# Convolution with generated weights, then a tanh-shrink MLP: a check of the softmax sums on chip, and a general version behind a branch

## The chip, the cores and the metric

The kernel runs on one core of a Trainium2 chip. A core has five engines with a queue of instructions each: PE (matrix multiply), DVE (vector), ACT (scalar and activation functions), POOL (general purpose) and SP (which here issues transfers). They run side by side and wait for each other through semaphores. The metric is the device time of one execution in microseconds; the profile is of one execution of its own.

## The reference

Per token and head, seven raw weights are turned into a softmax, which weighs the seven latest tokens of that head's channel group. The result goes through a two-layer MLP whose activation is h - tanh(h).

```python
batch, seq, d_model = (8, 4096, 192); kernel_size = 7; n_heads = 8; d_ff = 2048
x = randn(batch, seq, d_model) * 0.1
weight_gen = randn(batch, seq, n_heads, kernel_size) * 0.3

w = weight_gen - np.max(weight_gen, axis=-1, keepdims=True)
w = np.exp(w)
w = w / (np.sum(w, axis=-1, keepdims=True) + 1e-09)
x_pad = np.concatenate([np.zeros((B, pad, D)), x], axis=1)
x_unf = x_pad[:, idx, :].reshape(B, S, K, H, group)      # idx: the 7 latest tokens
out = np.einsum('bshk,bskhg->bshg', w, x_unf).reshape(B * S, D)
h = out @ w_in
g = h - np.tanh(h)
return g @ w_out                                          # (32768, 192) float32
```

## The kernel before

The 32768 tokens are cut into 32 superblocks of 1024 tokens (`TOK`), numbered n = 0 to 31. In a superblock each of the 128 partitions holds eight tokens in a row (`J = 8`). For each superblock:

1. `weight_gen` and `x` are loaded (`load_wg`, `load_x`, on SP's queue). `softmax_exp` takes the exponential in place on ACT. The row maximum of the reference is not subtracted.
2. `softmax_sum` (lines 179 to 187) adds the seven exponentials of each token and head on DVE into a tile `zsum`: 64 sums per partition and superblock, from 448 numbers; in the steady part it is done in two halves of 32 sums from 224 numbers. `softmax_recip`, `softmax_norm` and `softmax_norm_ramp` take reciprocals of them, also on DVE, and scale the exponentials.
3. `products` multiplies `x` with the weights, mostly on POOL, with DVE's help (`help`, lines 250 and 251). The seven products of a token are added partly by transfers with addition, partly by PE.
4. PE transposes and adds the products (`conv_sums`, line 384), and ACT copies the result to `convT` (line 410).
5. The first matrix multiply (`gemm1`, lines 422 to 445) runs over 16 f tiles of 128 of the 2048 hidden channels. For each f tile PE makes `ph` (line 427, six matmuls: three chunks of channels, two row halves of 64), ACT takes the tanh into `th` (line 440), and DVE subtracts into `gt`, in bfloat16 (line 441). `ph` lives in a PSUM pool of three buffers, `psum_h`; the transposes' `pc` and the last superblock's `po2` take slots of the same ring. `th` has three buffers too.
6. The second matrix multiply (`out_stream`, line 495) runs one superblock behind: its matmuls, in pairs of two row halves, are interleaved with the first's of the next superblock. How many pairs follow each f tile is written out in `plan["pairs"]` (`STEADY`, line 682). ACT copies the sums to `out_sb` (line 514) and SP stores a whole superblock at once (line 518).

After the last superblock's f tiles nothing is left to interleave with. `gemm2_last` (lines 529 to 559) then runs the second multiply of superblock 31 by itself, token block by token block (j = 0 to 7): 32 matmuls into a slot of `psum_h` (line 538), a copy of one half by ACT (line 551), an addition by DVE (line 552), and after every second block a store by SP (line 554).

All of this stands under `tc.manual_schedule()` (line 564): on each engine the instructions run in the order in which the program writes them. So the place of a call in the loop of lines 707 to 768 is its place in the engine's queue. In that loop f tile k of superblock n issues first `gemm1(n, k)`, with its subtraction on DVE; what a later line of the same pass puts on DVE runs after the subtraction of f tile k and before that of f tile k + 1. Sums, halves of sums and normalizations of a coming superblock are put into the passes n = 1 to 27; from n = 28 on there is no coming superblock left for which they would be done (`soft`, line 712, is empty).

`psum_h` and all other pools are entered on `ctx` and live until the kernel ends. The program has no branch.

Of the kernel before, what the change touches and what calls it, by code (L numbers as in the profile page):

```python
# [8 lines left out]
FP32 = mybir.dt.float32  # L9
BF16 = mybir.dt.bfloat16  # L10

ACT = mybir.ActivationFunctionType
AX = mybir.AxisListType


@with_exitstack
def kernel(
# [20 lines left out]
    JH = J // 2  # L38
    HT = TOK // 2
    NSB = S // TOK  # L40
    NTOT = B * NSB
    NFT = F // P
    NC = D // R
    KA, KH = 4, 2
    PART = (2, 3)
    TWO_SUMS = (13, 14, 15, 16, 17, 18, 19, 20, 21, 22, 23, 24, 25, 26, 27, 28, 29, 30, 31)
    AHEAD = 4
# [11 lines left out]
    assert NFT == 2 * J, "one token block of the second matmul per pair of f tiles"  # L59

    const = ctx.enter_context(tc.tile_pool(name="const", bufs=1))
    xpool = ctx.enter_context(tc.tile_pool(name="xpool", bufs=2))
    wgpool = ctx.enter_context(tc.tile_pool(name="wgpool", bufs=3))
    papool = ctx.enter_context(tc.tile_pool(name="papool", bufs=3))
# [113 lines left out]

    def softmax_sum(n, j0=0, j1=J):

        if j0 == 0:
            zsum_of[n] = wgpool.tile([P, J * H], FP32, name="zsum")
        nc.vector.reduce_sum(  # L183
            out=zsum_of[n][:, j0 * H : j1 * H],
            in_=e_of[n][:, j0:j1].rearrange("p j h k -> p (j h) k"),
            axis=AX.X,
        )

    def softmax_recip(n, j0=0, j1=J):
        if j0 == 0:  # L190
            zr_of[n] = wgpool.tile([P, J * H], FP32, name="zr")
        nc.vector.reciprocal(zr_of[n][:, j0 * H : j1 * H], zsum_of[n][:, j0 * H : j1 * H])

    def softmax_norm(n, bank):

        wsm = softmax_tile()
        zr_v = bank[:, 512 - J * H : 512]
        nc.vector.reciprocal(zr_v, zsum_of[n][:])  # L198

        def finish():  # L200
            scale(nc.vector, wsm[:], e_of[n], zr_v)

        wsm_of[n] = (wsm, None, None, None)
        return finish

    def softmax_norm_ramp(n, bank):

        softmax_sum(n)
        wsm = softmax_tile()
        zr_v = bank[:, 512 - J * H : 512]  # L210
        nc.vector.reciprocal(zr_v, zsum_of[n][:])  # L211
# [14 lines left out]
        wsm_of[n] = (wsm, wsm_v, None, None)  # L226

    def scale(eng, wsm, e_t, zr):
        return eng.tensor_mul(  # L229
# [248 lines left out]
    half = {}  # L478
# [50 lines left out]
    def gemm2_last(j, f0=0, f1=NFT):  # L529

        n = NTOT - 1
        if f0 == 0:
            half[j] = psum_h.tile([P, 2, HT], FP32, name="po2", tag="ph")
        po = half[j]
        col = (j % 2) * HT + (j // 2) * P
        for f in range(f0, f1):
            for r in range(2):
                nc.tensor.matmul(  # L538
                    po[:, r, 0:D],
                    lhsT=g_of[n][f][r * R : (r + 1) * R, col : col + P],  # L540
                    rhs=w_out[r * R : (r + 1) * R, f, :],
                    start=(f == 0),
                    stop=(f == NFT - 1),
                )
        if f1 < NFT:
            return
        if j == 0:
            out_of[n] = opool.tile([P, J, D], FP32, name="out_sb")
        out_sb = out_of[n]
        ot = tpool.tile([P, D], FP32, name="ot", tag="th")  # L550
        nc.scalar.activation(out=ot[:], in_=po[:, 0, 0:D], func=ACT.Copy)
        nc.vector.tensor_add(out_sb[:, j, :], po[:, 1, 0:D], ot[:])
        if j % 2 == 1:
            nc.sync.dma_start(
                out=out[n * TOK : (n + 1) * TOK, :].rearrange("(p j) e -> p j e", p=P)[
                    :, j - 1 : j + 1, :
                ],
                in_=out_sb[:, j - 1 : j + 1, :],
            )
# [147 lines left out]
    for n in range(1, NTOT):  # L707
        more = n < NTOT - 1
        finish = []
        plan = FIRST if n == 1 else DOUBLE if n in DOUBLE_IN else APART if n in APART_IN else STEADY  # L710

        soft = [m for m in (n + 3 if n <= AHEAD else n + 4,) if m < NTOT]
        for f in range(NFT):
            ph = gemm1(n, f)
            if n == 1:
                if f == 1:
                    load_wg(5)
                if f == 5:
                    softmax_exp(4)
                steps = ((softmax_sum, 3), (softmax_recip, 3), (softmax_sum, 4))  # L720
                for at, (step, m, h) in zip(plan["sums"], [s + (h,) for s in steps for h in (0, 1)]):
                    if f == at:
                        step(m, h * JH, (h + 1) * JH)
                if f == 5:
                    wsm_of[3] = (softmax_tile(), None, e_of[3], zr_of[3])
                    rest = products(3)
            elif f == 1:
                if soft:
                    softmax_exp(soft[0])
                if n + 2 < NTOT:  # L730
                    rest = products(n + 2)
            if n == AHEAD and f == 4:
                softmax_exp(n + 4)
            if n > 1:
                for h, at in enumerate(plan["sums"]):
                    if soft and f == at:
                        softmax_sum(soft[0], h * JH, (h + 1) * JH)
            if n == AHEAD:
                for at, (step, h) in zip(EXTRA, [(s, h) for s in (softmax_sum, softmax_recip) for h in (0, 1)]):
                    if f == at:  # L740
                        step(n + 4, h * JH, (h + 1) * JH)
                if f == EXTRA[-1]:
# [24 lines left out]
            if f == (9 if n == 1 else 1) and n <= STORE_FIRST:  # L767
                loads(n)
# [3 lines left out]
    gemm2_last(0, J, NFT)  # L772
    for j in range(1, J):
        gemm2_last(j)


# [28 lines left out]
```

## Time and profile before

| | us |
|---|---|
| median of 3 runs | 746.48 (745.1 to 747.17) |
| span of the profiled execution | 743.4 |
| PE busy in it | 722.3 (97%) |
| DVE busy | 687.4 (92%) |
| ACT busy | 638.8 (86%) |
| POOL busy | 654.5 (88%) |
| `gemm1`'s subtractions on DVE (line 441), 512 of 1.217 us | 601.6 |
| sums on DVE (line 183), 61 of 0.387 us in the mean | 23.6 |
| matmuls of the last superblock's second multiply (line 538), 256 | 11.2 |

The span runs from the first to the last instruction that the profile shows; the runs' device time also holds what lies around it. A line of the profile's list of groups names line, engine, operation, output<-inputs, shapes and count; then the busy time and the mean in ns of one; then the idle time of the engine just before these instructions and who ended most of it. "PEld" is the loading of weights into PE, which overlaps its matmuls. A name with a q, as SPq, is an engine's sequencer: it waits and issues, and the engine itself is not busy. The chain that ended last is followed backwards from the last instruction, at each step to what released it.

### The profile page before, as it was taken

The page shows a single profiled execution, that of the slowest core. Times are in us where ns is not written, and L with a number is a line of the kernel's source. Part 1 is how long each engine was busy: PE and PEld are TensorE (multiplying, and loading weights), DVE is VectorE, ACT ScalarE, POOL GpSimd, SP SyncE. Part 2 cuts the span into 40 slices and gives each one's busy share as a digit, 9 for nine tenths or more (in the row PEclk, how much of TensorE's full clock was granted, in tenths as well). Part 3 has the DMA queues.
Part 4 walks back from the last instruction along what each step waited for, and adds up shares of the span by engine and source line. Part 5 has one row for each costly group of instructions (what it writes and reads, how often), then busy time and mean ns, then how long its engine had stood idle before and what let it go on. Part 6 is the DMA issues. An engine that isn't in the chain of part 4 may idle for free.

```text
span 743.4 us, 30037 instructions
## 1 busy us (share of the span) xinstructions
PE 722.3 (97%) x13616; PEld 556.5 (75%) x13616; DVE 687.4 (92%) x723; ACT 638.8 (86%) x872; POOL 654.5 (88%) x163
## 2 busy tenths in 40 slices
PE   3899999999999999999999999999999999999997
PEld 2477777778777777777777777777777777877777
DVE  7999899999999999999999999999999999988893
ACT  4888888888888888989889999898998989888882
POOL 7999999999999999999999999999999999991000
PEclk9899999999999999999999999999999999999999
DMA  8925367766567668878777977877887877776112
GB/s 236 245 46 161 135 172 185 195 179 149 124 183 184 183 185 224 210 199 203 166 202 209 236 186 204 178 195 205 221 209 195 192 181 194 193 149 110 45 45 86
DMA packets 34269, 130.06 MB, mean 175 GB/s; under 512 B 4591, under 2 KB 9439, under 8 KB 30174
## 3 DMA queue, kind: packets, MB, share of 16 engines
q0 software_dynamic: 19424, 51.12, 40.4%
q1 hardware_dynamic: 14718, 77.03, 27.6%
q8 instruction: 106, 1.74, 0.9%
q14 instruction: 21, 0.17, 0.1%
HBM read 54.52 MB, written 25.17 MB: 107 GB/s over the span
## 4 chain that ended last, share of the span: by engine, by line
PE 92%; DVE 5%; ACT 1%; issue 1%; DMA 1%; SPq 0%; DVEq 0%
PE ph L427 43%; PE obank L495 43%; PE pc L384 4%; DVE gt L441 3%; PE po L538 1%; ACT th L440 1%; DVE pa L299 1%; DMA wg_t<-in_weight_gen_dram 1%; DVE zsum L183 0%; SPq L134 0%; ACT convT L402 0%; DVE obank L211 0%; DVE pa L251 0%; DVE pb L299 0%; SPq L144 0%
## 5 line engine op out<-in xcount | busy, mean ns | idle before, releaser
L441 DVE TENSOR_TENSOR gt<-ph,th 128x1024 bf16<-128x1024 f32 x512 | 601.6, 1217 | 33.4 <-ACT th L440 23.2
L440 ACT ACTIVATE th<-ph 128x1024 f32<-128x1024 f32 x512 | 512.1, 1025 | 69.2 <-PE ph L427 60.3
L427 PE MATMUL ph<-convT,w_in 64*128 64x512 bf16 x3072 | 415.1, 379 | 5.3 <-DVE gt L441 3.3
L495 PEld LDWEIGHTS <-gt 64*128 64x128 bf16 x7936 | 355.6, 94 | 80.6 <-issue 6.3
L495 PE MATMUL obank<-w_out,gt 64*128 64x192 bf16 x7936 | 408.0, 243 | 0.9 <-issue 0.8
L299 POOL TENSOR_TENSOR pa<-x_t,wsm 128x2688 bf16<-128x2688 f32 (+3 forms) x68 | 338.9, 5232 | 0.2
L299 POOL TENSOR_TENSOR pb<-x_t,wsm 128x4608 bf16<-128x4608 f32 (+2 forms) x33 | 283.8, 8601 | 0.7 <-ACT wsm L221 0.5
L427 PEld LDWEIGHTS <-w_in 64*128 64x128 bf16 x3072 | 163.0, 94 | 86.0 <-issue 18.3
L514 ACT ACTIVATE out_sb<-obank 128x192 f32<-128x192 f32 x248 | 81.3, 328 | 11.2 <-PE obank L495 10.3
L410 ACT ACTIVATE convT<-pc 128x1024 bf16<-128x1024 f32 (+1 forms) x62 | 50.1, 810 | 2.9 <-PE pc L384 2.7
L236 POOL DMA_DIRECT2D pa<-pb x28 | 36.0, 1284 | 13.7 <-POOL pb L299 9.1
L384 PEld LDWEIGHTS <-pa 64*128 64x128 bf16 x2064 | 41.5, 100 | 6.8 <-DVE pa L299 1.1
L236 POOL DMA_DIRECT2D pa<-pa x21 | 34.7, 1651 | 9.6 <-DMA pa<-pb 8.9
L384 PE MATMUL pc<-ident,pa 64*128 64x64 bf16 x1968 | 41.2, 191 | 1.8 <-POOL pa L299 0.9
L183 DVE TENSOR_REDUCE zsum<-wg_t 128x32 f32<-128x224 f32 (+1 forms) x61 | 23.6, 387 | 2.9 <-ACT wg_t L169 2.9
L169 ACT ACTIVATE wg_t<-wg_t 128x448 f32<-128x448 f32 x32 | 18.2, 570 | 6.3 <-DMA wg_t<-in_weight_gen_dram 6.2
L251 DVE TENSOR_TENSOR pa<-x_t,ph 128x384 bf16<-128x384 f32 x34 | 18.8, 554 | 2.0 <-DVE ph L250 0.3
L229 DVE TENSOR_TENSOR wsm<-wg_t,pc 128x448 f32<-128x448 f32 x27 | 16.8, 621 | 2.5
L198 DVE RECIPROCAL pc<-zsum 128x64 f32<-128x64 f32 x27 | 14.9, 550 | 0.0
L384 PE MATMUL pc<-ident,pb 64*128 64x64 bf16 x216 | 4.9, 206 | 9.0 <-POOL pb L299 9.0
L384 PEld LDWEIGHTS <-pb 64*128 64x128 bf16 x288 | 6.3, 106 | 9.5 <-POOL pb L299 9.0
L538 PE MATMUL po<-w_out,gt 64*128 64x192 bf16 x256 | 11.2, 243 | 0.0
(27 smaller groups left out, 56.8 us busy)
## 6 DMA issues: line engine op xcount, KB each, us to landing
x_t<-in_x_dram SPq DMA_DIRECT2D x31, 1344.0 KB, 7.9
pa<-pb POOLq DMA_DIRECT2D x28, 1152.0 KB, 9.5
out_dram<-out_sb SPq DMA_DIRECT2D x31, 768.0 KB, 3.9
pa<-pa POOLq DMA_DIRECT2D x21, 768.0 KB, 7.2
wg_t<-in_weight_gen_dram SPq DMA_DIRECT2D x32, 224.0 KB, 7.1
x_t<-in_x_dram SPq DMA_DIRECT2D x1, 768.0 KB
w_out<-in_moe_w_out_dram POOLq DMA_DIRECT2D x1, 768.0 KB, 9.5
out_dram<-out_sb SPq DMA_DIRECT2D x4, 192.0 KB, 3.0
```

Of the source, the lines that this page charges most:

```text
L183: nc.vector.reduce_sum(out=zsum_of[n][:, j0 * H : j1 * H], in_=e_of[n][:, j0:j1].rearrange("p j h k -> p (j h) k"), axis=AX.X,)
L236: return nc.gpsimd.dma_start(out=out.rearrange("p k j d -> p k (j d)"), in_=in_.rearrange("p k j d -> p k (j d)"), accum_op=mybir.AluOpTyp ...
L251: nc.vector.tensor_mul(pa[:, 0:KH, j, :].rearrange("p k (h g) -> p k h g", h=H), bass.AP(tensor=x_v.tensor, offset=x_v.offset + j * D, ap= ...
L299: return eng.tensor_mul(prod(k0, k1)[:, :, j0:j1].rearrange("p k j (h g) -> p k (j h) g", h=H), bass.AP(tensor=x_v.tensor, offset=x_v.offs ...
L384: nc.tensor.matmul(pc[r][:, col : col + R] if home else pc[:, r, col : col + R], lhsT=prods[c][gi][r * R : (r + 1) * R, 2 * j : 2 * j + 2] ...
L410: last_conv[0] = nc.scalar.activation(out=out, in_=pc[:, :, 0:cols].rearrange("p r (cj t) -> p r cj t", t=R), func=ACT.Copy,)
L427: nc.tensor.matmul(ph[:, r, :], lhsT=w_in[r * R : (r + 1) * R, c, f * P : (f + 1) * P], rhs=convT[r * R : (r + 1) * R, c, :], start=(c == ...
L440: last_act[0] = nc.scalar.activation(out=th[:], in_=ph_f, func=ACT.Tanh)
L441: last_sub[0] = nc.vector.tensor_sub(gt[:], ph_f, th[:])
L495: mm = nc.tensor.matmul(po[:, 0:D], lhsT=g_of[n][f][r * R : (r + 1) * R, col : col + P], rhs=w_out[r * R : (r + 1) * R, f, :], start=(r == ...
L514: last_act[0] = nc.scalar.activation(out=out_sb[:, j, :], in_=po[:, 0:D], func=ACT.Copy)
L538: nc.tensor.matmul(po[:, r, 0:D], lhsT=g_of[n][f][r * R : (r + 1) * R, col : col + P], rhs=w_out[r * R : (r + 1) * R, f, :], start=(f == 0 ...
```

## The change

- `zsum`, a tile per superblock from a ring of three, becomes `zall`, one tile that keeps the sums of all 32 superblocks. Sums and reciprocals write and read it in the same places.
- New: `watch_sums(i)` takes the maximum and the minimum over the sums of eight superblocks (512 numbers per partition) on DVE. It is called in the passes n = 28 to 31, after f tile 8.
- New: `judge_sums` reduces the four maxima and minima to one each, compares them with 1e30 and 1e-30, and adds the two flags into a bfloat16 column; five small DVE instructions, in the pass n = 31 after f tile 10.
- New: `count_flags` adds the flags of all partitions with one matmul into a slot of `psum_h`, and DVE copies the count to an integer, `verdict`. It is called after token block 2 of the last superblock.
- All pools but `const` and the manual schedule are now closed after the last token block. Then every engine loads `verdict` into a register, its bounds are checked, and a branch runs the new function `guarded` if it is above zero. That function computes the whole output again in a general and plainly ordered way, with the row maximum, in a loop over the eight batches. With the given inputs the sums lie near 7 and the branch is not taken.

```diff
+def guarded(tc, x, weight_gen, out, ident, w_in, w_out):
...
+        tc.For_i(0, B, 1) as b,
+    ):
+        for s in range(S // TOK):
...
+            nc.vector.reduce_max(out=z[:], in_=w_v, axis=AX.X)
+            nc.vector.tensor_sub(w_v, w_v, z_v)
+            nc.scalar.activation(out=w_v, in_=w_v, func=ACT.Exp)
+            nc.vector.reduce_sum(out=z[:], in_=w_v, axis=AX.X)
...
+            for f in range(NFT):
...
+                nc.scalar.activation(out=th[:], in_=ph_f, func=ACT.Tanh)
+                nc.vector.tensor_sub(gt[:], ph_f, th[:])
...
+            nc.sync.dma_start(out=to.rearrange("o (p j) e -> (o p) j e", p=P), in_=out_sb[:])
...
+    LARGE, SMALL = 1e30, 1e-30
...
+    ordinary = ExitStack()
+    ctx = ordinary
...
-    zsum_of = {}
+    zall = const.tile([P, NTOT, J * H], FP32, name="zall")
+    extremes = const.tile([P, 2, 4], FP32, name="extremes")
+    flag = const.tile([P, 3], FP32, name="flag")
+    flag_bf = const.tile([P, 1], BF16, name="flag_bf")
+    ones_bf = const.tile([P, 1], BF16, name="ones_bf")
+    nc.vector.memset(ones_bf[:], 1.0)
+    verdict = const.tile([1, 1], mybir.dt.int32, name="verdict")
...
-        if j0 == 0:
-            zsum_of[n] = wgpool.tile([P, J * H], FP32, name="zsum")
         nc.vector.reduce_sum(
-            out=zsum_of[n][:, j0 * H : j1 * H],
+            out=zall[:, n, j0 * H : j1 * H],
...
+    def watch_sums(i):
+        some = zall[:, i * (NTOT // 4) : (i + 1) * (NTOT // 4)].rearrange("p n z -> p (n z)")
+        nc.vector.reduce_max(out=extremes[:, 0, i : i + 1], in_=some, axis=AX.X)
+        nc.vector.tensor_reduce(
+            out=extremes[:, 1, i : i + 1], in_=some, axis=AX.X, op=mybir.AluOpType.min
+        )
+
+    def judge_sums():
+        nc.vector.reduce_max(out=flag[:, 0:1], in_=extremes[:, 0], axis=AX.X)
+        nc.vector.tensor_reduce(
+            out=flag[:, 1:2], in_=extremes[:, 1], axis=AX.X, op=mybir.AluOpType.min
+        )
+        nc.vector.tensor_scalar(
+            out=flag[:, 0:1], in0=flag[:, 0:1], scalar1=LARGE, scalar2=None, op0=mybir.AluOpType.is_gt
+        )
+        nc.vector.tensor_scalar(
+            out=flag[:, 1:2], in0=flag[:, 1:2], scalar1=SMALL, scalar2=None, op0=mybir.AluOpType.is_lt
+        )
+        nc.vector.tensor_add(flag_bf[:], flag[:, 0:1], flag[:, 1:2])
+
+    def count_flags():
+        tally = psum_h.tile([P, 2, HT], FP32, name="tally", tag="ph")
+        nc.tensor.matmul(tally[0:1, 0, 0:1], lhsT=flag_bf[:], rhs=ones_bf[:], start=True, stop=True)
+        nc.vector.tensor_copy(verdict[:], tally[0:1, 0, 0:1])
...
-    ctx.enter_context(tc.manual_schedule())
+    scheduled = ExitStack()
+    scheduled.enter_context(tc.manual_schedule())
...
+            if n >= NTOT - 4 and f == 8:
+                watch_sums(n - (NTOT - 4))
+            if n == NTOT - 1 and f == 10:
+                judge_sums()
...
     for j in range(1, J):
         gemm2_last(j)
+        if j == 2:
+            count_flags()
+    scheduled.close()
+    ordinary.close()
...
+    beyond = nc.values_load(verdict[0:1, 0:1], min_val=0, max_val=2 * P)
+    with tc.If(beyond > 0):
+        guarded(tc, x, weight_gen, out, ident, w_in, w_out)
```

More of the change, by code (lines that the diff above doesn't have):

```diff
@@ L13 @@
 AX = mybir.AxisListType
+def guarded(tc, x, weight_gen, out, ident, w_in, w_out):
+    nc = tc.nc
+    B, S, D = x.shape
+    H, K = weight_gen.shape[2], weight_gen.shape[3]
+    G = D // H
+    P = nc.NUM_PARTITIONS
+    R, J, HALO = P // 2, 8, K - 1
+    TOK, JH, NC = P * J, J // 2, D // R
+    HT = TOK // 2
+    NFT = w_in.shape[2] // P
+    with (
+        tc.tile_pool(name="g_in", bufs=1) as gin,
+        tc.tile_pool(name="g_prod", bufs=1) as gprod,
+        tc.tile_pool(name="g_th", bufs=2) as gth,
+        tc.tile_pool(name="g_gt", bufs=1) as ggt,
+        tc.tile_pool(name="g_ph", bufs=2, space=bass.MemoryType.PSUM) as gph,
+        tc.tile_pool(name="g_po", bufs=2, space=bass.MemoryType.PSUM) as gpo,
+        tc.For_i(0, B, 1) as b,
+    ):
+        for s in range(S // TOK):
+            s0 = s * TOK
+            rows = x[bass.ds(b, 1)]
+            x_t = gin.tile([P, HALO + J, D], FP32, name="gx")
+            nc.sync.dma_start(
+                out=x_t[:, HALO:], in_=rows[:, s0 : s0 + TOK].rearrange("o (p j) d -> (o p) j d", p=P)
+            )
+            nc.sync.dma_start(
+                out=x_t[1:P, 0:HALO],
+                in_=rows[:, s0 + J - HALO : s0 + TOK - HALO].rearrange("o (p j) d -> (o p) j d", p=P - 1)[
+                    :, 0:HALO
+                ],
+            )
+            if s:
+                nc.sync.dma_start(out=x_t[0:1, 0:HALO], in_=rows[:, s0 - HALO : s0])
+            else:
+                nc.vector.memset(x_t[0:1, 0:HALO], 0.0)
+            w_t = gin.tile([P, J, H, K], FP32, name="gw")
+            nc.sync.dma_start(
+                out=w_t[:],
+                in_=weight_gen[bass.ds(b, 1), s0 : s0 + TOK].rearrange(
+                    "o (p j) h k -> (o p) j h k", p=P
+                ),
+            )
+            w_v = w_t[:].rearrange("p j h k -> p (j h) k")
+            z = gin.tile([P, J * H], FP32, name="gz")
+            z_v = z[:].rearrange("p (n o) -> p n o", o=1).to_broadcast([P, J * H, K])
+            nc.vector.reduce_max(out=z[:], in_=w_v, axis=AX.X)
+            nc.vector.tensor_sub(w_v, w_v, z_v)
+            nc.scalar.activation(out=w_v, in_=w_v, func=ACT.Exp)
+            nc.vector.reduce_sum(out=z[:], in_=w_v, axis=AX.X)
+            nc.vector.tensor_scalar_add(z[:], z[:], 1e-9)
+            nc.vector.reciprocal(z[:], z[:])
+            nc.vector.tensor_mul(w_v, w_v, z_v)
+            prod = gprod.tile([P, K, J, D], BF16, name="gprod")
+            for k in range(K):
+                nc.vector.tensor_mul(
+                    prod[:, k].rearrange("p j (h g) -> p (j h) g", h=H),
+                    x_t[:, k : k + J].rearrange("p j (h g) -> p (j h) g", h=H),
+                    w_t[:].rearrange("p j h (k o) -> p k (j h) o", o=1)[:, k].to_broadcast([P, J * H, G]),
+                )
+            conv = gin.tile([P, NC, HT], BF16, name="gconv")
+            for c in range(NC):
+                pc = gph.tile([P, 2, HT], FP32, name="gpc", tag="gph")
+                for k in range(K):
+                    for j in range(JH):
+                        for r in range(2):
+                            nc.tensor.matmul(
+                                pc[:, r, j * R : (j + 1) * R],
+                                lhsT=prod[r * R : (r + 1) * R, k, 2 * j : 2 * j + 2].rearrange(
+                                    "p j (u c) -> p c (j u)", c=NC
+                                )[:, c],
+                                rhs=ident[r * R : (r + 1) * R, r * R : (r + 1) * R],
+                                start=(k == 0 and j == 0),
+                                stop=(k == K - 1 and j == JH - 1),
+                            )
+                nc.scalar.activation(
+                    out=conv[:, c].rearrange("p (j r t) -> p r j t", r=2, t=R),
+                    in_=pc[:, :, 0 : JH * R].rearrange("p r (j t) -> p r j t", t=R),
+                    func=ACT.Copy,
+                )
+            gts = []
+            for f in range(NFT):
+                ph = gph.tile([P, 2, HT], FP32, name="gph", tag="gph")
+                for c in range(NC):
+                    for r in range(2):
+                        nc.tensor.matmul(
+                            ph[:, r, :],
+                            lhsT=w_in[r * R : (r + 1) * R, c, f * P : (f + 1) * P],
+                            rhs=conv[r * R : (r + 1) * R, c, :],
+                            start=(c == 0),
+                            stop=(c == NC - 1),
+                        )
+                th = gth.tile([P, TOK], FP32, name="gth")
+                ph_f = ph[:].rearrange("p r t -> p (r t)")
+                gt = ggt.tile([P, TOK], BF16, name=f"ggt{f}")
+                nc.scalar.activation(out=th[:], in_=ph_f, func=ACT.Tanh)
+                nc.vector.tensor_sub(gt[:], ph_f, th[:])
+                gts.append(gt)
+            out_sb = gin.tile([P, J, D], FP32, name="gout")
+            for j in range(J):
+                po = gpo.tile([P, 2, HT], FP32, name="gpo")
+                col = (j % 2) * HT + (j // 2) * P
+                for f in range(NFT):
+                    for r in range(2):
+                        nc.tensor.matmul(
+                            po[:, r, 0:D],
+                            lhsT=gts[f][r * R : (r + 1) * R, col : col + P],
+                            rhs=w_out[r * R : (r + 1) * R, f, :],
+                            start=(f == 0),
+                            stop=(f == NFT - 1),
+                        )
+                half = gth.tile([P, D], FP32, name="ghalf")
+                nc.scalar.activation(out=half[:], in_=po[:, 0, 0:D], func=ACT.Copy)
+                nc.vector.tensor_add(out_sb[:, j, :], po[:, 1, 0:D], half[:])
+            to = out.rearrange("(b t) e -> b t e", b=B)[bass.ds(b, 1), s0 : s0 + TOK]
+            nc.sync.dma_start(out=to.rearrange("o (p j) e -> (o p) j e", p=P), in_=out_sb[:])
@@ L191, in softmax_recip @@
             zr_of[n] = wgpool.tile([P, J * H], FP32, name="zr")
-        nc.vector.reciprocal(zr_of[n][:, j0 * H : j1 * H], zsum_of[n][:, j0 * H : j1 * H])
+        nc.vector.reciprocal(zr_of[n][:, j0 * H : j1 * H], zall[:, n, j0 * H : j1 * H])
     def softmax_norm(n, bank):
@@ L197, in softmax_norm @@
         zr_v = bank[:, 512 - J * H : 512]
-        nc.vector.reciprocal(zr_v, zsum_of[n][:])
+        nc.vector.reciprocal(zr_v, zall[:, n])
         def finish():
@@ L210, in softmax_norm_ramp @@
         zr_v = bank[:, 512 - J * H : 512]
-        nc.vector.reciprocal(zr_v, zsum_of[n][:])
+        nc.vector.reciprocal(zr_v, zall[:, n])
         if n == 2:
@@ L226, in softmax_norm_ramp @@
         wsm_of[n] = (wsm, wsm_v, None, None)
+    def watch_sums(i):
[3 more added lines that the diff above has]
+            out=extremes[:, 1, i : i + 1], in_=some, axis=AX.X, op=mybir.AluOpType.min
+        )
+    def judge_sums():
+        nc.vector.reduce_max(out=flag[:, 0:1], in_=extremes[:, 0], axis=AX.X)
+        nc.vector.tensor_reduce(
+            out=flag[:, 1:2], in_=extremes[:, 1], axis=AX.X, op=mybir.AluOpType.min
+        )
+        nc.vector.tensor_scalar(
+            out=flag[:, 0:1], in0=flag[:, 0:1], scalar1=LARGE, scalar2=None, op0=mybir.AluOpType.is_gt
+        )
+        nc.vector.tensor_scalar(
+            out=flag[:, 1:2], in0=flag[:, 1:2], scalar1=SMALL, scalar2=None, op0=mybir.AluOpType.is_lt
+        )
+        nc.vector.tensor_add(flag_bf[:], flag[:, 0:1], flag[:, 1:2])
[3 more added lines that the diff above has]
+        nc.vector.tensor_copy(verdict[:], tally[0:1, 0, 0:1])
     def scale(eng, wsm, e_t, zr):
```

## The prediction

> **What bounds the kernel now.** I read the page's busy shares and chain first, then the busy time of each superblock, then the order of instructions inside one, then the last microseconds. The first fence is from the page, the second is the table of stretches, one per superblock from 28 on (columns: length, then busy time and count for PE, PEld, DVE, ACT, POOL, then granted clock, DMA share, GB/s).
>
> ```profile
> span 743.4 us, 30037 instructions
> ...
> PE 92%; DVE 5%; ACT 1%; issue 1%; DMA 1%; SPq 0%; DVEq 0%
> ...
> L441 DVE TENSOR_TENSOR gt<-ph,th 128x1024 bf16<-128x1024 f32 x512 | 601.6, 1217 | 33.4 <-ACT th L440 23.2
> L440 ACT ACTIVATE th<-ph 128x1024 f32<-128x1024 f32 x512 | 512.1, 1025 | 69.2 <-PE ph L427 60.3
> L427 PE MATMUL ph<-convT,w_in 64*128 64x512 bf16 x3072 | 415.1, 379 | 5.3 <-DVE gt L441 3.3
> ```
>
> ```profile
> 640.55:662.40 21.85, 21.85 (x405) 17.60 (x402) 20.03 (x20) 19.31 (x26) 21.31 (x6) 1.00 0.61 127
> 662.40:684.30 21.90, 21.90 (x406) 17.28 (x403) 19.49 (x18) 19.41 (x27) 10.33 (x3) 1.00 0.69 142
> 684.30:706.11 21.81, 21.81 (x406) 16.87 (x402) 18.94 (x16) 19.32 (x27) 0.00 (x0) 1.00 0.22 61
> 706.11:726.20 20.09, 20.04 (x326) 14.82 (x321) 17.97 (x16) 17.06 (x24) 0.00 (x0) 1.00 0.11 42
> ```
>
> PE sets the end: 92% of the chain, and no idle time in superblocks 28 to 30, whatever DVE has to do. DVE has 1.8 to 2.9 us free in each of them. But DVE also returns PE's buffers: the subtraction of line 441 is the last reader of `ph`, which has three buffers, so the first matmul of f tile k waits for the subtraction of tile k-3. PE's largest named wait is that one (3.3 us in all). So the question is not how much DVE idles in a superblock, but how late a subtraction may be at the place where work is put in. I took that from the timeline of superblock 28, around the place:
>
> ```profile
> 654.12 3.47 DVE L441 TENSOR_TENSOR gt<-ph,th 128x1024 bf16<-128x1024 f32 x3
> ...
> 655.70 0.83 PE L427 MATMUL ph<-convT,w_in 64*128 64x512 bf16 x6
> ```
>
> The first of those subtractions is tile 9's; at 1.215 us it ends at 655.33. The matmuls of tile 12 start at 655.70, so 0.37 us later. In superblocks 29, 30 and 31 the same distance is 0.43, 0.38 and 0.37 us. The smallest distance anywhere is 0.05 us (tile 9 of superblock 28, where PE did wait), so 0.05 is the hand-over itself and the spare time is 0.32, 0.38, 0.33 and 0.32 us. The subtractions of tiles 9 to 11 run back to back (each starts 0.08 us before the one ahead ends), so DVE makes up nothing in between.
>
> **The change, part by part.**
>
> *Sums kept.* The rows and counts of the sums and reciprocals stay; `zsum` becomes `zall`. Writer and readers are all on DVE, and the sum's row shows 0.0 us idle before the steady form, so no buffer wait goes away: nothing gained or lost. The new memset of `ones_bf` (nearest row: `zero`, 0.22 us) falls into DVE's idle 2.88 us before the first sum; without that cover it would be 0.2.
>
> *`watch_sums`, four times two reductions after the subtraction of tile 8 of superblocks 28 to 31.* The rows of reductions:
>
> ```profile
> L183 DVE TENSOR_REDUCE zsum<-wg_t 128x32 f32<-128x224 f32 x58 | 21.8, 375 | 0.0
> L250 DVE COPY ph<-wsm 128x16 f32<-128x16 f32 x34 | 6.4, 190 | 1.6 <-DVE gt L441 0.5
> L183 DVE TENSOR_REDUCE zsum<-wg_t 128x64 f32<-128x448 f32 x3 | 1.8, 614 | 2.9 <-ACT wg_t L169 2.9
> ```
>
> 224 more elements cost 239 ns, or 1.07 ns each, over a fixed 136 ns. A reduction over 512 elements is then 136 + 546 = 682 ns, less the 0.08 us overlap: 0.60, and the two 1.20 us. Behind them on DVE stands the subtraction of tile 9, and for it waits PE's tile 12, with the spare times above. PE stalls 1.20 less 0.32, 0.38, 0.33, 0.32: 0.88 + 0.82 + 0.87 + 0.88 = 3.45 us. PE has no idle time in which to take this back; later DVE gaps (0.66 us at tile 14, 0.40 at 15) only bring DVE level again before the next superblock. Bounds: if the count of outputs mattered, 512 could cost as the 224 form, 2 x 0.295 = 0.59 and a stall of some 1.0 in all; if each were 0.75, 4.6; if PE could make it up, 0.
>
> The Trainium skill (VectorE: DVE Perf Modes, The perf-mode tier table) says that tensor_reduce runs at the 1x rate for every type, from SBUF as from PSUM. The slope above agrees, and by the page no cheaper reduction is to be hoped for; the sum stays.
>
> *`judge_sums` in superblock 31 after tile 10.* Two reductions of four elements at 0.14 us and three single-column operations by the copy row's 0.19: 0.85 us. DVE is then 2.05 us late at tile 11. Tile 14's matmuls wait for that subtraction; their distance is 0.93, so 0.88 spare, and PE is by then 0.86 us late itself: 2.05 - 0.88 - 0.86 = 0.3 us of stall. Tile 15 has 0.98 us and does not stall again. Bounds 0 and 0.85.
>
> *`count_flags`.* One weight load and one matmul between token blocks 2 and 3 of the last superblock. PE's row there is back to back. Bounds: a matmul step of 0.04 us and load plus matmul in full, 0.09 + 0.24. No row shows a matmul over 128 rows after ones over 64, so I take the middle, 0.15. The tally also takes a `ph` slot, so block 3 reuses block 1's buffer; that was free at 732.41, and block 3 starts at 732.65, so 0.2 us remain. The copy to `verdict` goes into DVE's 0.96 us gaps.
>
> *The end.* After its last instruction every engine now reads a word of `verdict`, checks it, and jumps over the general version. What the end looks like (a timeline line, a group of SP's waits, a row of the DMA issues):
>
> ```profile
> 740.36 0.33 SPq L554 DMA_DIRECT2D out_dram<-out_sb  x1
> ...
> SPq L800 <- DMA out_dram<-out_sb: 1.1, 1, 1.1
> ...
> out_dram<-out_sb SPq DMA_DIRECT2D x4, 192.0 KB, 3.0
> ```
>
> SP issues the last store until 740.69, steps through waits 0.06 us apart, idles 1.1 us until it has landed at 742.2, and the closing handshakes run to 743.4. So only 1.1 us of new work on SP is covered. No row shows a register read, a jump or a stall for code. Read: between 0.02 (a wait's own step) and 3.0 (issue to landing of a store); I take 0.6, the time by which the engine's first 48-byte reads on the instruction queue precede the span. Check and branch: two steps, 0.1. Code beyond the jump: between 0.75 (the closing code's 8 KB packet starts 0.3 us after the last instruction and takes 0.45) and 6.0 (two fetches, one behind the other, at 3.0); I take one at 3.0, the nearest transfer somebody waits for. In all 3.7. If the branch runs while the store is in flight, 1.1 is covered and 2.6 are added; if it stands behind the store's landing, because the general version writes `out` too, 3.7. I take 3.1. Bounds: 0.02 + 0.1 + 0.75 is under 1.1, so 0; and 3.0 + 0.1 + 6.0 = 9.1. POOL and PE wait too, but they have been done for longer.
>
> The Trainium skill (Runtime: NRT & Kernel Launch, Instruction fetch mechanics) warns that a taken branch to a target outside the two resident pages stalls for a fetch. Here the straight-line code is loaded in 106 packets of 16 KB and some of 8 KB and nothing in the trace waits for them, so the trace can neither confirm nor deny it. By the rule the fetch term must not be left out; by the trace alone it could be nothing, and the sum would be lower by 3.0 less the cover. The DMA page of the skill (DMA: Bandwidth & Descriptors) gives a tensor_load a floor near 600 ns; no run here shows one yet.
>
> Sum: 3.45 + 0.3 + 0.15 + 3.1 = 7.0 us. The profiled execution goes from 743.4 to 750.4; the median of the runs, 746.48, lies 3.1 us above that span, and the same 7.0 gives 753.5.
>
> **The rivals.**
>
> *A heavier end (0.20).* The general version's code lies between the branch and the close, and if its tiles, loop and stores bring an all-engine handshake (0.95 us by the closing ones, 742.45 to 743.40) and a second fetch, the end costs 3.7 + 3.0 + 0.95 = 7.7 instead of 3.1: 758. For it: five engines, each with its own jump. Against: only the last engine's chain counts.
>
> *DVE absorbs the reductions (0.15).* The superblocks where they stand have no sums or normalizations left, and 1.8 to 2.9 us of idle time. If the order allowed that, only 0.15 + 3.1 remain: 749.7. Against it stand the 0.32 us at tile 12.
>
> *No change, within 0.3% (0.10).* All additions fit under what is idle already, the end under the landing of the last store. Its price is a few steps of 0.06 us, 0.3 us with the tally: 746.8. It decides where read, branch and fetch stay under SP's 1.1 us and PE can regain a stall within the superblock. For it: the DVE totals and the bounds' low ends. Against it: PE busy in all of 21.8 us.
>
> *It doesn't do what it says (0.02).* If the branch is taken, 32 unpipelined superblocks follow, each at least 16 subtractions of 1.2 us: over 600 us more. The inputs give sums of seven exponentials near 7, so no.
>
> **How the numbers follow.** My forecast has 0.53, for 753.5 (its own range 750 to 756.5). The range of 8 in 10 goes down to 748.5, which leaves out most of the no-change case, and up to 759, which holds most of the heavier end. About 0.3% (2.2 us) is what a measurement can tell from no change. Slower by more: the forecast, the heavier end, most of the third case, 0.87. Within: 0.11. Faster has no mechanism but a shifted address layout: 0.02.
>
> **What would show it.** In the changed profile: reductions of 0.68 us over 512 elements; a PE wait of some 0.9 us for the subtraction at tile 12 of each of the last four superblocks, these 22.7 us long; one of 0.3 near tile 14 of the last. Then, after the last store's issue, register reads and a gap of some 3 us before the closing handshakes, with instruction packets in it. I am wrong if superblocks 28 to 31 keep 21.8 us, or if the handshakes begin at the landing as before.

## The result, and the profile after

| | before | after |
|---|---|---|
| median, us | 745.82 (4 runs) | 750.74 (4 runs, 750.47 to 752.2) |
| ratio | | 1.0072 [1.0056, 1.0087] |
| span of the profiled execution | 743.4 | 748.7 |
| superblocks 28, 29, 30 | 21.85, 21.90, 21.81 | 22.92, 22.88, 22.87 |
| start of superblock 31 to the start of ACT's last copy | 33.50 | 34.57 |
| end of the last store's issue to end of span | 2.71 | 4.39 |

The change costs 4.9 us by the medians and 5.3 us between the two profiled executions. These split into parts: 1.07 + 0.98 + 1.06 us in superblocks 28 to 30, 1.07 in 31, 1.68 at the end, less 0.6 us by which superblock 28 happened to start earlier (639.9 against 640.6). That last part is scatter: the same program run again started it at 640.5.

The page of the changed kernel, the lines that answer to those shown before (its line 580 is 427 of before, 593 is 440, 594 is 441):

```profile
span 748.7 us, 30084 instructions
...
PE 89%; DVE 7%; ACT 2%; issue 1%; DMA 0%; DVEq 0%
...
L594 DVE TENSOR_TENSOR gt<-ph,th 128x1024 bf16<-128x1024 f32 x512 | 601.4, 1218 | 32.4 <-ACT th L593 22.9
L593 ACT ACTIVATE th<-ph 128x1024 f32<-128x1024 f32 x512 | 512.3, 1026 | 72.3 <-PE ph L580 62.3
L580 PE MATMUL ph<-convT,w_in 64*128 64x512 bf16 x3072 | 414.9, 379 | 7.9 <-DVE gt L594 5.9
```

PE's share of the chain falls by three hundredths and DVE's rises by two: the chain now passes through DVE where PE waits for it, and that wait went from 3.3 to 5.9 us. Groups that do the same work cost the same as before. The view shows less than the superblocks lose: it counts a wait from the end of the matmuls ahead, which leaves 0.63 to 0.69 us of each of the four waits at tile 12 (2.7 us), and it leaves out gaps of under 0.15 us. The same stretches as before, cut at the starts of superblocks 28 to 31 (columns: length, then busy time and count of PE, PEld, DVE, ACT, POOL; clock, DMA share, GB/s):

```profile
639.94:662.86 22.92, 22.10 (x406) 17.59 (x403) 21.04 (x22) 19.38 (x26) 22.38 (x6) 1.00 0.63 130
662.86:685.74 22.88, 22.12 (x406) 16.86 (x403) 20.50 (x20) 19.43 (x27) 9.26 (x3) 1.00 0.68 140
685.74:708.61 22.87, 22.05 (x405) 16.92 (x402) 19.95 (x18) 19.37 (x27) 0.00 (x0) 1.00 0.14 45
```

Where PE had no idle time it now has 0.8 us in each superblock, and DVE still has 1.9 to 2.9 us free. The timeline of superblock 28 shows the place:

```profile
652.37 1.22 DVE L594 TENSOR_TENSOR gt<-ph,th 128x1024 bf16<-128x1024 f32 x1 [0.15 <-ACT th L593]
...
653.51 0.68 DVE L357 TENSOR_REDUCE extremes<-zall 128x1 f32<-128x512 f32 x1
653.75 0.83 PE L580 MATMUL ph<-convT,w_in 64*128 64x512 bf16 x6
...
654.10 0.68 DVE L358 TENSOR_REDUCE extremes<-zall 128x1 f32<-128x512 f32 x1
...
654.69 2.35 DVE L594 TENSOR_TENSOR gt<-ph,th 128x1024 bf16<-128x1024 f32 x2
655.96 0.82 PE L580 MATMUL ph<-convT,w_in 64*128 64x512 bf16 x6 [0.69 <-DVE gt L594]
```

The two reductions stand between the subtractions of tiles 8 and 9 (652.37, 654.69). The subtraction of tile 9 ends at 655.91, and 0.05 us later PE starts tile 12: 2.21 us after tile 11 (653.75), where it was 1.35 before.

A second, smaller delay stands two tiles later. PE's matmuls from tile 13 to tile 14 of superblock 28, before:

```profile
657.01 0.83 PE L427 MATMUL ph<-convT,w_in 64*128 64x512 bf16 x6
657.66 0.65 PE L384 MATMUL pc<-ident,pa 64*128 64x64 bf16 x32
...
658.90 0.85 PE L427 MATMUL ph<-convT,w_in 64*128 64x512 bf16 x6
```

and after:

```profile
657.26 0.83 PE L580 MATMUL ph<-convT,w_in 64*128 64x512 bf16 x6
658.22 0.65 PE L537 MATMUL pc<-ident,pa 64*128 64x64 bf16 x32
...
659.35 0.83 PE L580 MATMUL ph<-convT,w_in 64*128 64x512 bf16 x6
```

The transposes now start 0.96 us after tile 13 instead of 0.65, and tile 14 comes after 2.09 us instead of 1.89. In superblocks 28 to 30 of the changed kernel the transposes start 0.05 us after the subtraction of tile 11 ends (658.17 here), with PE idle for 0.13 us ahead of them; before, PE had no such gap.

The end, in the instructions of the branch's line on each engine's queue (count, then duration in ns, first and last start):

```profile
L941 SPq EVENT_SEMAPHORE  x8: 17/17/17, 744.8 to 746.6; - x8
L941 POOLq COMPARE_BRANCH  x1: 45/45/45, 737.8 to 737.8; - x1
L941 PEldq COMPARE_BRANCH  x1: 3650/3650/3650, 742.8 to 742.8; - x1
...
L941 DVEq COMPARE_BRANCH  x1: 72/72/72, 744.2 to 744.2; - x1
L941 SPq COMPARE_BRANCH  x1: 50/50/50, 744.3 to 744.3; - x1
...
L941 DVEq EVENT_SEMAPHORE  x1: 21/21/21, 747.5 to 747.5; - x1
```

Three things are to be seen. PE's branch takes 3.65 us. DVE's is over in 0.07, but its next step comes 3.28 us after the branch's start. SP's comes 0.5 us after; then SP steps through eight semaphores, one per lane of its transfers, and the last ones wait until the last store has landed (746.4). The last store was issued from 743.93, so it is seen to land after 2.49 us, where it took 1.87 before. From there to SP's last step ahead of the closing handshakes it is 1.42 us (746.42 to 747.84), where it was 0.28 (742.23 to 742.51): before, most of SP's steps lay ahead of the landing, and now most of them stand behind it, with a pause of 0.40 us among them.

### The profile page after: what moved, and what is told of

It is laid out like the page before. It is cut to its first block, busy times and chain, and to the rows that moved or that the text cites. A ratio compares the mean times of both kernels' runs of the same rounds, so it can differ in the third digit from the quotient of the medians.

```text
span 748.7 us, 30084 instructions
## 1 busy us (share of the span) xinstructions
PE 723.7 (97%) x13617; PEld 556.7 (74%) x13617; DVE 692.1 (92%) x738; ACT 639.2 (85%) x872; POOL 654.7 (87%) x163
## 4 chain that ended last, share of the span: by engine, by line
PE 89%; DVE 7%; ACT 2%; issue 1%; DMA 0%; DVEq 0%
PE obank L648 42%; PE ph L580 42%; DVE gt L594 5%; PE pc L537 4%; PE po L691 1%; ACT th L593 1%; DVE pa L452 1%; DVE pb L452 0%; DMA wg_t<-in_weight_gen_dram 0%; DVE extremes L357 0%; DVE extremes L358 0%; DVE zall L309 0%; DVE obank L337 0%; DVE wsm L382 0%; DVE obank L382 0%
## 5 line engine op out<-in xcount | busy, mean ns | idle before, releaser
L309 DVE TENSOR_REDUCE zall<-wg_t 128x32 f32<-128x224 f32 (+1 forms) x61 | 23.7, 388 | 2.8 <-ACT wg_t L297 2.8
L324 DVE RECIPROCAL pc<-zall 128x64 f32<-128x64 f32 x27 | 14.9, 551 | 0.0
```

Of the source, the lines that this page charges most:

```text
L309: nc.vector.reduce_sum(out=zall[:, n, j0 * H : j1 * H], in_=e_of[n][:, j0:j1].rearrange("p j h k -> p (j h) k"), axis=AX.X,)
```

## The experiments

Each ran in five rounds beside the kernel before, and the ratio is to the kernel before on the same chip. The first four rows are from one chip, the changed kernel's repeat among them; the other rows are from three other chips, so a difference between one of them and the changed kernel is a difference between chips too. The changed kernel itself has 1.0072 in the result and 1.0087 here. The column "31 to last copy" goes to the start of ACT's last copy.

| kernel | ratio [95%] | superblocks 28 to 30 | 31 to last copy | end |
|---|---|---|---|---|
| changed, again | 1.0087 [1.0074, 1.0100] | 22.92, 22.87, 22.88 | 34.57 | 4.36 |
| no branch | 1.0054 [1.0042, 1.0067] | 22.92, 22.88, 22.87 | 34.58 | 2.71 |
| branch only | 1.0032 [1.0020, 1.0044] | 21.86, 21.87, 21.82 | 33.50 | 4.55 |
| moved | 1.0032 [1.0020, 1.0044] | 21.82, 21.87, 21.81 | 33.72 | 4.38 |
| half moved | 1.0048 [1.0033, 1.0063] | 22.28, 22.28, 22.28 | 33.98 | 4.75 |
| double | 1.0157 [1.0142, 1.0172] | 24.10, 24.06, 25.45 | 35.76 | 4.88 |
| tally in halves | 1.0096 [1.0068, 1.0125] | 22.91, 22.88, 22.88 | 34.57 | 4.54 |
| tiny arm | 1.0048 [1.0035, 1.0061] | 22.92, 22.88, 22.87 | 34.57 | 2.61 |
| fall through | 1.0095 [1.0081, 1.0110] | 22.92, 22.88, 22.87 | 34.57 | 5.18 |
| arm on POOL | 1.0077 [1.0061, 1.0093] | 22.92, 22.87, 22.88 | 34.57 | 4.19 |
| moved, arm on POOL | 1.0026 [1.0016, 1.0036] | 21.82, 21.87, 21.81 | 33.72 | 4.42 |
| the same, small arm | 1.0023 [1.0011, 1.0035] | 21.86, 21.86, 21.82 | 33.72 | 3.53 |

### The changed kernel again, and its two halves

> The changed kernel again, beside the others on one chip. Both theories: about 4.9 us over before (4 to 6.5). In the trace superblocks 28 to 30 some 22.9 us long, 31 with a PE wait of 0.87 us at tile 12, and 4.4 us from the end of the last store's issue to the end of the span (before: 2.7). If superblock 28 starts near 640 again, 0.6 us earlier than in the one profile of before, the difference of the early part belongs to the kernel; if it starts elsewhere, it is scatter between executions.

Measured: 5.9 us over before (751.32 against 745.42). The superblocks and the end repeat to 0.05 us, while the early part moves by over half a microsecond from execution to execution (superblock 28 starts at 640.46 here; between 639.9 and 641.6 in this and the next three kernels). So parts of the trace are compared below, and totals only with their intervals.

```diff
-    beyond = nc.values_load(verdict[0:1, 0:1], min_val=0, max_val=2 * P)
-    with tc.If(beyond > 0):
-        guarded(tc, x, weight_gen, out, ident, w_in, w_out)
```

> Left out: the read of the verdict, the branch and the general version; sums, reductions, flags and tally stay. Theory A (PE waits at tile 12 for the subtraction behind the reductions, 4.0 us, tally 0.2, end 1.7): 1.7 us less than the changed kernel, 2.7 us from the last store's issue to the end, superblocks as long as with the change. Theory C (the branch and the general version's code make most of the loss, also outside the span): within 1 us of before.

Measured: the end is back at 2.71 us and the superblocks stay long. By the ratios 0.0033, or 2.5 us, less than the changed kernel, with intervals of about 1 us each. Theory C falls: most of the loss stays without the branch.

```diff
+    nc.vector.memset(verdict[:], 0)
...
-            if n >= NTOT - 4 and f == 8:
-                watch_sums(n - (NTOT - 4))
-            if n == NTOT - 1 and f == 10:
-                judge_sums()
...
-        if j == 2:
-            count_flags()
```

> Left out: the reductions, flags and tally; the verdict is set to 0 at the start, and read and branch stay. Theory A: 1.7 us over before, all of it after the last store; superblocks 28 to 31 at 21.8 to 21.9 us. Theory C: 3 to 5 us over before.

Measured: superblocks as before, the end 4.55 us: 1.84 more than before, and 2.4 us (1.5 to 3.3) by the ratio. The two halves add up to the whole, and `zall` itself costs nothing that shows in a superblock. DVE's branch is remarkable here:

```profile
L936 DVEq COMPARE_BRANCH  x1: 72/72/72, 739.9 to 739.9; - x1
...
L936 DVEq EVENT_SEMAPHORE  x1: 21/21/21, 740.5 to 740.5; - x1
```

Its next step comes 0.58 us after the branch instead of 3.28, although the whole general version stands behind it, and yet the end is not shorter. SP's last step ahead of the closing handshakes comes 3.88 us after the start of the last store's issue, in the changed kernel 3.91: the landing and SP's steps take that long by themselves. (The closing handshakes are 0.2 us longer here.) Why DVE goes on so soon was not settled; the page counts 725 instructions on DVE here, and 738 in the changed kernel.

### The place of the reductions

```diff
-            if n >= NTOT - 4 and f == 8:
-                watch_sums(n - (NTOT - 4))
+            if n >= NTOT - 4 and f in ((1, 3) if n == NTOT - 1 else (13, 15)):
+                watch_sums(n - (NTOT - 4), f in (3, 15))
```

`watch_sums` now does one of the two, the minimum where its second argument is true.

> The same eight reductions, at other places: a maximum after tile 13 and a minimum after tile 15 of superblocks 28 to 30, where DVE idles 0.66 us before the next subtraction, and after tiles 1 and 3 of superblock 31, where a subtraction may be 0.4 us late. Theory A: no PE wait is left, superblocks of 21.8 to 21.9 us, 4.0 us less than the changed kernel, about 1.3 us over before. Theory B (DVE's added work costs by its amount, some 4.7 us, wherever it stands): as slow as the changed kernel, within 1 us.

The superblocks of the moved kernel:

```profile
641.47:663.29 21.82, 21.82 (x406) 16.82 (x403) 20.68 (x21) 19.33 (x27) 21.42 (x6) 1.00 0.62 128
663.29:685.16 21.87, 21.87 (x405) 16.85 (x402) 20.68 (x20) 19.38 (x27) 10.32 (x3) 1.00 0.73 149
685.16:706.97 21.81, 21.81 (x405) 16.88 (x402) 20.13 (x18) 19.33 (x27) 0.00 (x0) 1.00 0.19 55
```

DVE does as much as in the changed kernel (20.68 against 20.50 us in superblock 29), and PE has no gap: 21.87 busy of 21.87. The ratio falls from 1.0087 to 1.0032, 4.1 us. Theory B falls: the same work costs 4 us in one place and nothing in another. What is left in superblock 31, 0.22 us, is the tally. The expected 1.3 us over before was too low: the ratio gives 2.4 us (1.5 to 3.3), the parts of the trace 1.9 (0.22 and 1.67 at the end). It had been taken from the 5.3 us between the two profiled executions, which are 0.6 us too few by the early part.

The half-moved kernel keeps the maxima behind tile 8 and moves the minima:

> The four maxima stay behind tile 8, the four minima move behind tile 15 (superblock 31: tile 3). Theory A: 0.59 us of work against 0.33 us spare at tile 12 leaves a PE wait of some 0.26 us there and 0.2 us at tile 14 of superblocks 28 to 30: these 22.3 us long, in all 1.7 us of stall instead of 4.0, so 2.3 us less than the changed kernel. Theory B (by amount): as slow as the changed kernel.

Measured: 22.28 us in each of the three superblocks and a step from tile 11 to 12 of 1.63, 1.56, 1.66 and 1.66 us, that is 0.28, 0.22, 0.27 and 0.27 us of wait. The ratio is 0.0039 under the changed kernel's, 2.9 us. Its profiled execution lost some 8 us before superblock 16, so nothing is taken from its total.

```diff
             if n >= NTOT - 4 and f == 8:
                 watch_sums(n - (NTOT - 4))
+                watch_sums(n - (NTOT - 4))
```

> The eight reductions done twice at the same place, 1.18 us more on DVE in each of the last four superblocks. Theory A (what exceeds the spare 0.33 us at tile 12 becomes a PE wait in full): 4 x 1.18 = 4.7 us more than the changed kernel, superblocks 28 to 30 at 24.1 us, the wait at tile 12 about 2.05 us and the 0.2 us at tile 14 as before. Theory F (PE can make up part of a stall): less than 4 us more.

Measured: 24.10 and 24.06 us, 1.18 more than with two reductions, as expected, and 1.19 more in superblock 31. But superblock 30 took 25.45. The columns of these stretches are as above; the clock is the third from the right:

```profile
702.00:705.60 3.60, 1.82 (x33) 1.25 (x29) 3.60 (x7) 1.96 (x3) 0.00 (x0) 1.00 0.00 0
705.60:708.20 2.60, 2.50 (x23) 1.79 (x24) 2.30 (x3) 1.01 (x1) 0.00 (x0) 0.53 0.00 0
708.20:710.50 2.30, 2.30 (x60) 1.72 (x57) 1.23 (x1) 1.30 (x4) 0.00 (x0) 0.79 0.03 7
```

After an idle time of 1.87 us PE came back at half its clock for 3.4 us, which cost another 1.4 us (25.45 against 22.87 and 1.18). The idle times of 1.87, 1.82 and 1.87 us in the other three superblocks did not do that. The total rose by 0.0070 in the ratio, 5.2 us, against 4.7 expected; the two ratios are from different chips, and how many of the runs lost the 1.4 us is not known. By the superblocks theory F falls: PE made up nothing.

### The tally

```diff
-        nc.tensor.matmul(tally[0:1, 0, 0:1], lhsT=flag_bf[:], rhs=ones_bf[:], start=True, stop=True)
-        nc.vector.tensor_copy(verdict[:], tally[0:1, 0, 0:1])
+        for r in range(2):
+            nc.tensor.matmul(
+                tally[0:1, r, 0:1],
+                lhsT=flag_bf[r * R : (r + 1) * R],
+                rhs=ones_bf[r * R : (r + 1) * R],
+                start=True,
+                stop=True,
+            )
+        with nc.allow_low_precision(reason="a count of at most 256"):
+            nc.vector.reduce_sum(
+                out=verdict[:], in_=tally[0:1, :, 0:1].rearrange("p r o -> p (r o)"), axis=AX.X
+            )
```

> The tally as two matmuls over 64 rows each, in the row halves that all other matmuls use, added by DVE, instead of one over 128 rows. If the 0.21 us that token block 3 came late is the change from 64 to 128 rows and back: 0.08 us instead, so superblock 31's start to the last copy of ACT takes 34.45 us instead of 34.57. If it is the matmul itself: 34.6 or more. The total time cannot tell (0.1 us).

Measured: 34.57 us, the same as with one matmul of 128 rows; the total, with an interval of 1.0068 to 1.0125, says nothing. So the 0.2 us is not the change of the rows' number. What it is was not settled.

### The end

In the next kernel `guarded(...)` is replaced by `nc.vector.memset(once[:], 0.0)`.

> The branch stays, but the general version behind it is left out: one memset stands there. Theory D (the end is longer by SP's own steps after the landing: more lanes to wait for, and a landing 0.5 us later): reductions as with the change, and an end of 3.7 to 4.2 us after the last store's issue, at most 0.7 us less than the changed kernel. Theory E (the jump over far code sets the end): the target is near, no engine stalls at its branch, PE's branch takes 0.1 us instead of 3.6, and the end is back at 2.7 to 3.0 us, 1.4 to 1.7 us less than the changed kernel.

Measured: an end of 2.61 us, and the ratio 0.0039 under the changed kernel's, 2.9 us, of which the end shows 1.75. PE's branch takes 0.22 us, and DVE's next step follows after 0.23. That is theory E's number. But the kernel does not separate the two theories as it should have: with no transfers behind the branch, SP has no lanes to step through either, and its branch came ahead of the last store.

```diff
-    with tc.If(beyond > 0):
+    with tc.If(beyond > 0, preferred_fallthrough_block=False):
```

> The changed kernel, but the branch asked to fall through into the end when the sums are ordinary, the general version standing behind a taken branch. Theory E: no jump in this case, an end of 2.7 to 3.2 us, 1.2 to 1.7 us less than the changed kernel. Theory D: an end of 3.7 to 4.4 us, within 0.7 us of the changed kernel.

Measured: 5.18 us, outside both. The branch line shows why:

```profile
L941 PEldq COMPARE_BRANCH  x2: 95/1908/3722, 744.9 to 745.5; - x2
...
L941 DVEq COMPARE_BRANCH  x2: 51/53/55, 746.3 to 746.5; - x2
```

Every engine now branches twice. The first falls through to the semaphore steps, the second jumps over the general version after all, and PE's takes 3.72 us. On SP the second stands behind the landing, at 749.4. The far jump is not gone; it comes later.

To take SP's steps away and leave the jump, the general version's transfers were issued from POOL (`nc.sync.dma_start` replaced by `nc.gpsimd.dma_start` in `guarded`):

> The changed kernel, but the transfers of the general version are issued from POOL's queue instead of SP's. They are not executed in either case; what differs is which engine steps through the lanes' semaphores at the join. Theory D (SP's steps after the landing make the end long): an end of 3.3 to 3.8 us after the last store's issue instead of 4.4, the landing itself still some 0.5 us later than without a branch. Theory E (the jump and its fetch alone): 4.4 us as before.

Measured: 4.19 us, closer to theory E. Among SP's waits stands the reason:

```profile
SPq L968 <- DVEq L941: 2.0, 1, 2.0
```

SP's lane steps are gone, and it waits instead for DVE, which goes on 3.17 us after its branch. In the changed kernel the two chains end within 0.4 us of each other (DVE's next step at 747.46, SP's last at 747.84), so taking one away gains 0.2.

The two changes that helped were then put together.

> Both at once: the reductions at the places of the moved kernel, and the general version's transfers on POOL's queue. Theories A and D: superblocks of 21.8 to 21.9 us and an end of 3.3 to 3.8 us: 1.0 to 1.7 us over before, the least of all versions with the check and the branch. It is not expected below before, since the tally (0.2 us) and an end over 2.7 us stay.

Measured: 1.0026, 1.9 us over before. The superblocks are as expected; the end, 4.42 us, is not, since DVE's next step comes 3.40 us after its branch.

```diff
-        for s in range(S // TOK):
+        for s in range(1):
```

> The moved kernel with the transfers on POOL's queue, and three quarters of the general version left out: its loop body holds one superblock of a batch instead of four. Nothing of it is executed in either case; DVE's and ACT's code behind the branch is a quarter as long, PE's is still long. If DVE's jump (3.3 us from its branch to its next step in the kernel with four) is what ends last there: DVE's next step within 0.6 us of its branch, and an end of 3.2 to 3.7 us after the last store's issue instead of 4.4, now set by the landing and PE's jump. If the end is the same for any branch with its reads: 4.2 to 4.5 us as before.

Measured: DVE's and ACT's next steps 0.58 and 0.45 us after their branches, PE's branch still 3.51 us, and an end of 3.53. SP now waits for the store:

```profile
SPq L970 <- DMA out_dram<-out_sb: 1.9, 1, 1.9
```

So DVE's slow jump did end last in the kernel with four superblocks behind the branch and the transfers on POOL's queue, and most of what is left at the end over before is the landing: 2.8 us from issue, where the kernel before has 1.87. This version, which is not complete, costs 1.7 us by its ratio (0.8 to 2.6). Of the complete versions with check and branch, the moved ones are the best; none beats the kernel before.

## Why the prediction was right, and where it was not

The forecast was 7.0 us more, 753.5, with 748.5 to 759 as the range. Measured were 4.9 us more by the medians, 750.74, and 5.9 in the repeat; the parts of the trace, 3.39 + 0.6 + 0.21 + 1.68, add up to 5.9. Of the 2.8 us by which 753.5 is too high, 0.7 is the median of before, which fell from 746.48 to 745.82 with a fourth run. The sum is closer than its terms: 0.6 us that were left out make up for a part of what the flags and the end had too much.

**Sums kept: nothing.** Right: superblocks of the branch-only kernel are within 0.03 us of before.

**Reductions, 3.45 us at tile 12.** Right: 0.86 + 0.81 + 0.86 + 0.86 = 3.39 us. A reduction took 0.676 us against 0.682 worked out from two rows. The spare time read from the timeline of before decides to within 0.05 us at half, full and double the work. The prediction missed a smaller stall of the same kind: the step from tile 13 to 14 in superblocks 28 to 30 went from 1.89 to 2.09 us, 0.6 in all. Between them stand the transposes, whose `pc` takes a slot of the same ring and waits for tile 11's subtraction, by then 0.3 us later against PE than before. The prediction followed `ph` alone.

**Flags, 0.3 us.** None was seen: the step from tile 13 to 14 of superblock 31 stayed at 1.51 us. The five instructions delayed the next subtraction by 0.5 us, not 0.85: they take 0.145 to 0.162 us each and start 0.07 to 0.17 us apart, while the prediction had counted whole durations, three of them by a row of 16 columns.

**Tally, 0.15 us.** 0.21.

**The end, 3.1 us.** Mis-sized: 1.7. The failed step is "one at 3.0", put on SP in line with the read, and added to what SP's 1.1 us of idle time did not cover. The 3.0 fits what the fetch took, 3.3 us on DVE and 3.65 on PE, but by luck in part: it was the time of a store from issue to landing. SP had read `verdict` at 737.2, ahead of its last stores, and its own jump took 0.5 us. DVE's jump began with the last store's issue and ran beside the landing. So two chains run side by side: DVE's jump, then the handshake; and a landing 0.62 us later with 1.14 us more of SP's steps behind it. The second ends last, and with handshakes shorter by 0.08 it makes the 1.68; DVE is ready for the handshake 0.3 us ahead of SP. Each chain alone makes an end of over 4 us: the second in the branch-only kernel, where DVE's jump is short, the first in the kernel with the transfers on POOL's queue, where SP waits for DVE.

**The rivals.** The heavier end did not come: 1.7 us, not 7.7. That DVE absorbs the reductions is wrong at tile 8 and right at tiles 13 and 15 (in superblock 31 at tiles 1 and 3). No change, within 0.3%, is excluded for the changed kernel by both its intervals, 1.0056 to 1.0087 and 1.0074 to 1.0100. The branch was not taken: no general version is in the trace.

The Trainium skill's rule (Runtime: NRT & Kernel Launch, Instruction fetch mechanics), that a taken branch out of the resident code stalls for a fetch, agrees with most of what is seen, engine by engine: 2.6 to 3.4 us on ACT and DVE and 3.4 to 3.9 on PE where the code behind the branch is long, 0.2 to 0.6 where it is short. One jump does not fit the length of the code: DVE's in the branch-only kernel, 0.58 us over the whole general version. The floor near 600 ns for a `tensor_load` (the Trainium skill, DMA: Bandwidth & Descriptors, Latency and other measured facts) is a little high here: 0.46 to 0.60 us in all but one of the loads (0.74).

## What to carry to other kernels

An engine that is 10% idle can still hold up the bound one: read, at the very place, how late it may be before the next buffer is missed, and follow every user of that ring. The same instructions then cost 4 us or nothing, by where they stand. A conditional block that is never executed can still cost a jump on every engine at once, and only what ends last of those chains, of the transfers in flight and of the steps at the join counts.

## What was not expected of the hardware

- A stall can cost twice: after 1.87 us without work PE ran at half clock for 3.4 us, once in four such stalls of one execution. The half-moved kernel's profiled execution shows it once, far from the change: 2.31 us without work from 265.3 us, and half clock from 267.3 to 270.7. The stalls of 0.7 us at tile 12 never had this.
- A far jump comes with a later landing of the last store. In the kernels without a far jump all 16 parts of the last store have landed 1.86 us after its issue. In those with one, 13 or 14 have by 1.9 us, and the other two or three take 2.0 to 3.1 us, while packets of 8 and 16 KB on the instruction queues are moved. That these cause it is inferred from the coincidence in all runs with a far jump; it was not tried by itself.
